# Transposes of q and k for the unit three ahead, issued behind the transposes of x

## The chip, the cores and the metric

The kernel runs on one core of one Trainium2 chip. The core has five engines that run side by side, each through its own queue in order: TensorE (PE in the profile, with PEld for its weight loads), VectorE (DVE), ScalarE (ACT), GpSimd (POOL) and SyncE (SP). DMA transfers are issued by POOL and by SP here and are carried out by 16 DMA engines. The metric is the device time of one execution in microseconds, the median of several runs.

## The reference

Chunked attention on q, k and v of shape (8 batches, 8 heads, 576 positions, 64), with every chunk of 64 positions attending to itself alone, and then a gated feed-forward layer on the 4608 x 512 result:

```
scores = q_c @ k_c.T / sqrt(64)            # per batch, head and chunk: 64 x 64
attn   = softmax(scores)
x      = (attn @ v_c)   -> 4608 x 512      # tokens x (heads * 64)
h      = x @ w_in                          # 512 -> 2048
g      = h * sigmoid(beta * h)
out    = g @ w_out                         # 2048 -> 512, float32
```

## The kernel before

The 4608 tokens are cut into 18 units of 256. Two units make a block of 512, so there are nine blocks, and the loop over `j` from 1 to 8 goes through what is called stage j here. Stage j computes the hidden layer of block j (`emit_m`, 16 column groups, matmuls on L366), the output products of block j - 1 (`emit_prod`, L583; seven products in two halves each instead of eight, with sums of operands formed on VectorE by `emit_sum`, L430), and the attention of later units. In stages 3, 4 and 5 it is the attention of three units each: 8 to 10, 11 to 13, 14 to 16. Unit 17 follows in stage 6.

For each unit u the attention has these steps:

- `load_unit(u)`: POOL issues the loads of q and k of the unit (L104, tiles `qu` and `ku`, four buffers each) and of v (L118, tile `vbig`, a ring of sixteen parts). The loads convert float32 to float16.
- `emit_T(u)`, called T(u) below: for u >= 8, two DMA transposes on SP (L157), `kT<-ku` and then `qT<-qu`; the tiles kT and qT have three buffers each. At its end it calls `loads_to(u + 4)`, so the load of unit u + 4 is put on POOL's queue; that load overwrites the buffers that T(u) reads.
- `emit_sc(u)`, called sc(u): the score matmuls (L217) read qT and kT, then ScalarE takes the exponential (L223).
- `emit_pv(u)`: matmuls with v (L254).
- `emit_norm(u, s)` in two halves: reciprocals and products on VectorE (L286, L288, L276) and two small activations on ScalarE (L287) give x in float16 (`x16`, two buffers).
- `emit_xt_dma(u, s)`, called xt(u) for the two halves: a DMA transpose on SP each (L342, `xt<-x`) into the block's tile `xt`. `emit_m` of block j reads the transposed x of both units 2j and 2j + 1. So the first `emit_m` of stage 4 reads xt(8) and xt(9).

The outputs leave by DMAs on SP as well (L537, `out_dram<-osb`). ScalarE copies a product out of PSUM into one of four `osb` buffers (L600), VectorE adds a second product to it (L603), and `flush_stores` puts the store on SP's queue at the end of the next product. A copy that reuses a buffer waits until the buffer's earlier store has landed.

All of it is issued under a manual schedule: no planner moves anything. Each stage fills a list `items` of (place, priority, step), sorts it by place and then priority, and calls the steps in that order; each engine then works through its own part of the program in this order, and each instruction waits on semaphores for its inputs and for the buffer that it overwrites. The places are fractions of a stage. `ATT` gives for each unit its start a0 and its width w, and `att_items` makes the places of its steps out of them. In stage 3 the three units have a0 = 0.02, 0.35 and 0.68 and w = 0.33:

```
3: ((8, 0.02, 0.33), (9, 0.35, 0.33), (10, 0.68, 0.33)),
```

A step's place orders it among all the steps of its stage; on SP what counts is the order among the transposes and the stores alone. An SP instruction that waits holds up all that is behind it on SP.

Of the kernel before, what the change touches and what calls it, by code (L numbers as in the profile page):

```python
# [15 lines left out]
def kernel(  # L16
# [595 lines left out]
    with tc.manual_schedule():  # L612
# [96 lines left out]
        def att_items(u, a0, w):  # L709
            it = [(a0, 2, ("sc", u)), (a0 + 0.36 * w, 3, ("pv", u)), (a0 + 0.361 * w, 3, ("norm", u, 0)),  # L710
                  (a0 + (0.42 if u >= WV else 0.50) * w, 3, ("norm", u, 1))]
            if u >= WV:
                it.append((a0 + 0.005, 3, ("T", u + 3)))
            return it

        ATT = {2: ((6, 0.36, 0.27), (7, 0.60, 0.27)),
# [12 lines left out]
        for j in range(1, NB):  # L729
# [19 lines left out]
            else:  # L749
# [28 lines left out]
                for i, p in enumerate((1, 2, 6, 5, 7, 3, 4)):  # L778
                    for t in range(2):
                        w = 1.06 if j == NB - 1 else 0.98  # L780
# [15 lines left out]
                for u, a0, w in ATT.get(j, ()):  # L796
                    items += att_items(u, a0, w)
# [86 lines left out]
```

## Time and profile before

| | |
|---|---|
| time, median of 3 runs | 286.99 us (284.39 to 287.27) |
| the profiled execution | 286.72 us, span 284.9 us |
| mean granted TensorE clock | 0.975 |
| PE busy | 269.6 us (95%) |
| VectorE busy | 208.1 us (73%) |
| ScalarE busy | 165.1 us (58%) |
| GpSimd busy | 96.9 us (34%) |
| DMA packets' share, GpSimd's queue / SP's queue | 81.1% / 34.9% |
| PE waiting for `xt<-x` | 3.6 us, once |
| first product of stage 3, 4, 5, 6 on PE | 98.47, 127.40, 162.53, 192.32 us |

The span runs from the first to the last instruction, and the execution's time has 1.8 us around it. Times within the profile are microseconds from the start of the span. In the rows of the forty slices each digit is a share in tenths, for 7.1 us; PEclk is the clock granted to TensorE in tenths of full speed. The queues' shares are of the time of all 16 DMA engines; they can add up to more than 100%, since an engine can have packets of both queues under way. In a list in order of time a line gives the start, the length, the engine, the line of the program, the operation, what it writes and reads, and how many instructions are merged; in brackets the idle time before it and what ended it. A DMA's line on SP or POOL is the time of issuing it; its landing comes later and is given as the time from the start of the issue.

### The profile page before, as it was taken

To read this page: it belongs to the slowest core of one execution; us is meant where nothing else is said; L and a number is where in the kernel's file an instruction comes from. 1 tells how busy PE (TensorE), PEld (TensorE's weight loads), DVE (VectorE), ACT (ScalarE), POOL (GpSimd) and SP (SyncE) were. 2 spreads that over 40 slices of the span, in tenths; PEclk is the share of its full clock that TensorE was granted. 3 is DMA by queue.
4 is the path that set the end of the run, shared out by engine and by line. 5 is a ranking of instruction groups with operands and counts; after the bars stand their busy time and mean duration, and the time that the engine had idled before them with its cause. 6 is when DMAs were issued, how large, how long until landed. Compare 5 with 4: busy or idle time off the path is not lost.

```text
span 284.9 us, 7719 instructions
## 1 busy us (share of the span) xinstructions
PE 269.6 (95%) x3186; PEld 184.6 (65%) x3186; DVE 208.1 (73%) x389; ACT 165.1 (58%) x295; POOL 96.9 (34%) x124
## 2 busy tenths in 40 slices
PE   6589999899999999994999999999999999999995
PEld 2466445656756566662566666666787887788874
DVE  3557666799987587663676687669997989696961
ACT  3358506886555565652456565656657576848721
POOL 8864579489538709432434300000000000000000
PEclk9959999999999999996899999999999999999999
DMA  9999999999999999999999999623412102110223
GB/s 142 174 196 204 181 180 179 241 164 157 141 137 137 173 185 162 153 176 156 192 151 169 157 160 231 132 25 100 66 37 76 37 2 74 39 37 3 74 75 112
DMA packets 145955, 36.95 MB, mean 130 GB/s; under 512 B 130048, under 2 KB 145408, under 8 KB 145920
## 3 DMA queue, kind: packets, MB, share of 16 engines
q0 software_dynamic: 101216, 18.10, 81.1%
q1 hardware_dynamic: 44704, 18.37, 34.9%
q8 instruction: 25, 0.41, 0.6%
q14 instruction: 10, 0.08, 0.1%
HBM read 36.71 MB, written 9.44 MB: 162 GB/s over the span
## 4 chain that ended last, share of the span: by engine, by line
PE 59%; DMA 18%; DVE 10%; POOL 4%; ACT 4%; issue 3%; DVEq 0%; ACTq 0%; POOLq 0%
PE hps L366 22%; PE ya L583 12%; PE yb L583 10%; DMA ku<-in_k_dram 6%; DMA wout<-in_moe_w_out_dram 5%; PE acc L583 5%; PE qx L479 3%; ACT hq L511 3%; DMA win<-in_moe_w_in_dram 3%; PE qz L479 3%; DMA xt<-x 3%; DVE gt L354 2%; DVE gt L525 2%; POOL vbig L118 2%; PE sc L217 1%
## 5 line engine op out<-in xcount | busy, mean ns | idle before, releaser
L366 PE MATMUL hps<-xt,win 128*128 128x512 f16 (+1 forms) x504 | 114.5, 365 | 5.6 <-DMA xt<-x 3.6
L354 DVE SCALAR_TENSOR_TENSOR gt<-sg,hps 128x512 f16<-128x512 f32 (+1 forms) x113 | 69.1, 617 | 44.1 <-ACT sg L378 43.5
L378 ACT ACTIVATE sg<-hps,bt 128x512 f32<-128x512 f32 (+1 forms) x113 | 71.1, 635 | 49.6 <-PE hps L366 48.6
L366 PEld LDWEIGHTS <-win 128*128 128x128 f16 x504 | 49.2, 100 | 40.2 <-DMA xt<-x 3.9
L583 PEld LDWEIGHTS <-sm 128*128 128x128 f16 x512 | 49.3, 98 | 12.3 <-issue 0.3
L583 PEld LDWEIGHTS <-gt 128*128 128x128 f16 x384 | 37.1, 99 | 10.5 <-DVE gt L525 0.6
L118 POOL DMA_DIRECT2D vbig<-in_v_dram x40 | 34.1, 871 | 17.9 <-DMA ku<-in_k_dram 5.3
L104 POOL DMA_DIRECT2D qu<-in_q_dram x22 | 18.7, 861 | 25.9 <-DMA qT<-qu 9.2
L583 PE MATMUL ya<-wt,sm 128*128 128x256 f16 x200 | 26.0, 273 | 0.0
L104 POOL DMA_DIRECT2D ku<-in_k_dram x22 | 18.8, 872 | 11.8 <-DMA ku<-in_k_dram 6.1
L525 DVE TENSOR_SCALAR gt<-hq,rb 128x512 f16<-128x512 f32 x32 | 14.5, 482 | 7.5 <-ACT hq L511 6.5
L430 DVE TENSOR_TENSOR sm<-gt 128x2048 f16<-128x2048 f16 (+1 forms) x17 | 19.7, 1156 | 0.3
L511 ACT ACTIVATE hq<-hq,bs 128x256 f32<-128x256 f32 (+1 forms) x32 | 17.1, 611 | 1.8 <-DVE hq L504 1.8
L600 ACT COPY osb<-ya 128x512 f32<-128x512 f32 x18 | 10.6, 587 | 8.0 <-PE ya L583 7.6
L391 PE MATMUL ops<-wout,gt 128*128 128x512 f16 x64 | 14.5, 379 | 0.0
L583 PE MATMUL ya<-wout,gt 128*128 128x256 f16 x104 | 14.3, 284 | 0.0
L583 PE MATMUL yb<-wout,gt 128*128 128x256 f16 x104 | 13.9, 273 | 0.2
L239 ACT ACTIVATE et<-sc 128x1024 f16<-128x1024 f32 (+1 forms) x9 | 7.3, 833 | 11.4 <-PE sc L230 11.4
L479 PEld LDWEIGHTS <-ws 128*128 128x128 f16 x128 | 12.5, 98 | 2.0 <-issue 0.6
L583 PE MATMUL yb<-wt,sm 128*128 128x256 f16 x104 | 13.5, 273 | 0.1
L583 PE MATMUL yb<-wout,sm 128*128 128x256 f16 x104 | 13.5, 273 | 0.0
L375 ACT ACTIVATE sg<-hps,bs 128x512 f32<-128x512 f32 x13 | 8.8, 687 | 7.2 <-PE hps L366 7.2
(99 smaller groups left out, 344.4 us busy)
## 6 DMA issues: line engine op xcount, KB each, us to landing
out_dram<-osb SPq DMA_DIRECT2D x32, 256.0 KB, 3.0
vbig<-in_v_dram POOLq DMA_DIRECT2D x32, 128.0 KB, 8.0
qu<-in_q_dram POOLq DMA_DIRECT2D x20, 128.0 KB, 5.8
ku<-in_k_dram POOLq DMA_DIRECT2D x20, 128.0 KB, 7.1
win<-in_moe_w_in_dram POOLq DMA_DIRECT2D x8, 256.0 KB, 9.1
wout<-in_moe_w_out_dram POOLq DMA_DIRECT2D x4, 512.0 KB, 12.2
qu<-in_q_dram POOLq DMA_DIRECT2D x4, 256.0 KB, 6.3
ku<-in_k_dram POOLq DMA_DIRECT2D x4, 256.0 KB, 7.2
```

The lines of the kernel that those rows point to most:

```text
L104: nc.gpsimd.dma_start(out=tv[off:off + n, sp], in_=src[b, :, s:s + n, :].rearrange("h p d -> p h d"),)
L118: nc.gpsimd.dma_start(out=vbig[off:off + n, i % NV, :, 0:D], in_=v[b, :, s:s + n, :].rearrange("h p d -> p h d"),)
L354: nc.vector.scalar_tensor_tensor(out=gt_t[j][:, m, c0:c0 + n], in0=sg[:, 0:n], scalar=1.0, in1=hps[:, 0:n], op0=ALU.add, op1=ALU.mult,)
L366: nc.tensor.matmul(out=hps[:, 0:n], lhsT=w_in16[m // 2][:, kk, (m % 2) * 128:(m % 2) * 128 + 128], rhs=xr[:, c0 // CH:(c0 + n) // CH, 2 * ...
L378: nc.scalar.activation(out=sg[:, 0:n], in_=hps[:, 0:n], func=ACTF.Tanh, scale=bt[:, m:m + 1])
L391: nc.tensor.matmul(out=ops, lhsT=gt_t[j][:, kk, t * 128:(t + 1) * 128], rhs=w_out16[kk // 4][:, kk % 4, :], start=(kk == 0), stop=(kk == K ...
L430: nc.vector.tensor_tensor(out=sm[i][:, lo:hi, :], in0=a, in1=b, op=op)
L479: nc.tensor.matmul(out=dst[:, s, :], lhsT=lhsT, rhs=rhs, start=(p in (1, 2, 5) and s == 0 and kk == 0), stop=(s == 1 and kk == 1), skip_gr ...
L511: nc.scalar.activation(out=o, in_=src, func=ACTF.Silu, scale=bs[:, m:m + 1])
L525: nc.vector.tensor_scalar(out=gt_t[j][:, m, :], in0=hq[:, b].rearrange("p c q -> p (c q)"), scalar1=rb[:, m:m + 1], scalar2=None, op0=ALU. ...
L583: nc.tensor.matmul(out=dst, lhsT=lhsT, rhs=rhs, start=(p in (1, 2, 5) and kk == 0 and (t == 0 or last)), stop=(kk == 7 and (t == 1 or last ...
L600: nc.scalar.copy(out=o, in_=acc)
```

## The change

For units from 8 on (`WV` is 8), `att_items` puts T(u + 3) at another place of the list: at a0 + 0.45 w instead of a0 + 0.005. Before, that is just behind sc(u), which is at a0. Now it is behind the second half of the norm, at a0 + 0.42 w, and so behind the two xt(u), which are issued along with the halves of the norm.

```
             it = [(a0, 2, ("sc", u)), (a0 + 0.36 * w, 3, ("pv", u)), (a0 + 0.361 * w, 3, ("norm", u, 0)),
                   (a0 + (0.42 if u >= WV else 0.50) * w, 3, ("norm", u, 1))]
             if u >= WV:
-                it.append((a0 + 0.005, 3, ("T", u + 3)))
+                it.append((a0 + 0.45 * w, 3, ("T", u + 3)))
             return it
```

It concerns T(11) to T(17), which are issued by units 8 to 14; T(8), T(9) and T(10) are issued in stage 2, at places of their own. The order of the instructions on TensorE and on GpSimd is the same as before, and so is that on VectorE and ScalarE. On SP the order from T(10) on, with "st" for a store, is:

```
before: T10 T11 st xt8 st T12 xt9 T13 st xt10 st T14 st xt11 st T15 xt12 T16 st xt13 st T17 st xt14 st xt15 ...
after:  T10 st xt8 T11 st xt9 T12 st xt10 T13 st st xt11 T14 st xt12 T15 st xt13 T16 st st xt14 T17 st xt15 ...
```

More of the change, by code (lines that the diff above doesn't have):

```diff
@@ L712, in att_items @@
             if u >= WV:
-                it.append((a0 + 0.005, 3, ("T", u + 3)))
+                it.append((a0 + 0.45 * w, 3, ("T", u + 3)))
             return it
```

## The prediction

> **What bounds the kernel now.** I read the page first: its busy line and its forty slices, then the costliest groups, then the waits, then single stretches.
>
> ```profile
> PE 269.6 (95%) x3186; PEld 184.6 (65%) x3186; DVE 208.1 (73%) x389; ACT 165.1 (58%) x295; POOL 96.9 (34%) x124
> ...
> PEclk9959999999999999996899999999999999999999
> DMA  9999999999999999999999999623412102110223
> ...
> L366 PE MATMUL hps<-xt,win 128*128 128x512 f16 (+1 forms) x504 | 114.5, 365 | 5.6 <-DMA xt<-x 3.6
> ```
>
> PE is busy for 95% of the span, so only its gaps and its clock can be won. After the start the clock row dips once, in slices 19 and 20, and the group that reads x transposed (L366) has one long wait, 3.6 us for the transpose `xt<-x`. The DMA row is full until slice 25. The instructions in order of time on PE (start, length, line, operation, count, [idle before]) place the wait:
>
> ```profile
> 126.53 1.03 PE L366 MATMUL hps<-xt,win 128*128 128x512 f16 x4
> 127.40 1.04 PE L583 MATMUL ya<-wout,gt 128*128 128x256 f16 x8
> 132.01 1.89 PE L366 MATMUL hps<-xt,win 128*128 128x512 f16 x4 [3.58 <-DMA xt<-x]
> ```
>
> 127.40 is the first product of stage 4; the next matmul is the stage's first `emit_m`, which needs x of units 8 and 9, and it takes 1.89 us where its like takes 1.03. Busy time by stretches gives the clock:
>
> ```profile
> core 0: us, PE busy (x) PEld busy (x) DVE busy (x) ACT busy (x) POOL busy (x), PEclk, DMA share, GB/s
> ...
> 128.00:133.00 5.00, 1.42 (x7) 0.57 (x6) 1.92 (x2) 0.34 (x1) 1.59 (x3) 0.75 1.74 155
> 133.00:138.00 5.00, 5.00 (x79) 2.49 (x76) 1.82 (x2) 2.43 (x4) 1.57 (x2) 0.57 1.73 172
> ```
>
> A clock of 0.5 from 130.5 to 137.3 makes these means (2.5 of 5 us, then 4.3 of 5). The same view in order of time on SP shows why xt was late:
>
> ```profile
> 100.67 2.38 SPq L157 DMA_TRANSPOSE kT<-ku  x1
> 103.15 3.53 SPq L157 DMA_TRANSPOSE qT<-qu  x1
> 106.86 2.29 SPq L157 DMA_TRANSPOSE kT<-ku  x1
> 109.31 1.56 SPq L157 DMA_TRANSPOSE qT<-qu  x1
> 110.97 0.54 SPq L537 DMA_DIRECT2D out_dram<-osb  x1
> 111.61 3.57 SPq L342 DMA_TRANSPOSE xt<-x  x2
> 115.27 0.54 SPq L537 DMA_DIRECT2D out_dram<-osb  x1
> 115.97 3.96 SPq L157 DMA_TRANSPOSE kT<-ku  x1
> 120.03 3.26 SPq L157 DMA_TRANSPOSE qT<-qu  x1
> 123.38 2.67 SPq L342 DMA_TRANSPOSE xt<-x  x2
> ```
>
> These are T(10), T(11), a store, xt(8), a store, T(12), xt(9), where T(u) is kT and qT of unit u. SP runs back to back. VectorE finished x of unit 9 at 116.0 (its L276 pair: 114.86 + 1.15), yet xt(9) was issued at 123.4, behind T(12); its second half, issued at 124.8, landed 7.2 us later, at 132.0.
>
> **The price of that stall.** From first product to first product, stage 3 takes 127.40 - 98.47 = 28.93 us and stage 4 162.53 - 127.40 = 35.13. Stage 5 takes 29.79, of which 0.86 is the next stage's first `emit_m`, which comes ahead of the product there: 28.93 again. So stage 4 loses 6.20 us. That is 3.58 of idle PE, and 137.3 - 132.0 = 5.3 us at half clock, which loses 2.65: together 6.23.
>
> **The change, part by part.** No instruction is added or removed, and PE and POOL keep their order. On SP the seven pairs T(11) to T(17) go from just behind sc(u) to just behind the two xt of unit u.
>
> *xt(9), the gain.* After T(10) (end 106.7) come the store, ready long before, and xt(8), whose x was ready at 105.0 and 107.9: 107.4 to 111.0. T(11) follows, 4.0 us as now, then a store of 0.54: 115.6. x(9) is ready at 116.0, so xt(9) goes at 116.1, its second half at 117.5, and at 7.2 us it lands at 124.7. It is wanted at 128.27, behind the first product. Were T(11) as slow as T(12) now (7.3 us) and the landing that of xt(8) (9.1), it would be 129.4, 1.1 us late. So the idle and, with it, the half clock go: -6.2 us.
>
> *The T pairs, now later.* SP does the same work, so I start each where it started before, plus what now goes ahead of it: T(11) 106.86 + xt(8) 3.57 + store 0.54 = 111.0; T(12) + xt(9) 2.67 and 0.2 of waiting = 118.9; T(13) + xt(10) and a store = 130.0; T(14) + xt(11) and a store of 1.1 = 141.6; T(15) + xt(12) = 150.9; T(16) + xt(13) and a store = 163.7; T(17) + xt(14) and a store = 173.6. With each pair's own lead of kT (1.4 to 4.1 us) and its qT's time from issue to landing in the rows of that tile (7.7, 9.6, 8.4, 9.5, 9.5, 10.0, 4.6 us), they land at 121.2, 132.6, 141.7, 153.8, 163.7, 175.1 and 180.5. The score matmuls (L217) that read them stand now at 133.83, 144.2, 153.9, 164.4, 173.1, 182.8 and 193.3; the first comes at 129.2 without the stall, the others 6.2 earlier: 138.0, 147.7, 158.2, 166.9, 176.6, 187.1. Slack is 8.0, 5.4, 6.0, 4.4, 3.2, 1.5 and 6.6 us, so I take no cost. What hides them is PE's own work between T's issue and sc; where that fails, PE waits at sc. The worst landing of the trace, 10.0 us, is already in unit 16's sum; SP slower by 1 us per unit would make unit 16, five units on, 5 - 1.5 = 3.5 us late, my upper end. There is no gain below nothing, since PE waits for no qT from unit 8 on.
>
> *The loads behind them.* POOL's load of unit 15 overwrites what T(11) reads: it waited until 120.12 for an earlier load, and qT(11) now lands at 121.2, 1.1 us later. Load 14 is in flight until 131.7 (its last ku issued at 113.9, 17.8 us to landing), so the queue doesn't run dry: 0, or at most 1.1 us at ku(15), which lands at 147.1 and has 3.8 us before T(15) at 150.9. The last ku of unit 16 lands at 160.3, ahead of T(16) in the new order too; the later loads have their T landed well before POOL reaches them.
>
> *Stores behind the T.* Store of the third product's sum in stage 3 goes behind T(13), at 136.0, lands 6.8 later at 142.8; ScalarE reuses the buffer at 150.2 - 6.2 = 144.0. The one of stage 4 goes behind T(16), 169.7 as now, lands at 175.7 and is wanted at 179.1 - 6.2 = 172.9: ScalarE's copy stands 2.8 us. Behind it stand tanh activations; `emit_m` has four PSUM buffers 1.74 us apart and needs one about 2.7 us, so 4.2 us of cover. I take 0; uncovered it costs up to 2.8.
>
> *Sum.* The profiled execution took 286.72 us (span 284.9 and 1.8 around it), 0.1% under the median of 286.99. 286.72 - 6.2 = 280.5.
>
> **A rule that speaks against it.** T(12) held SP for 7.3 us (115.97 to 123.29). The Trainium skill (DMA: Bandwidth & Descriptors, Latency and other measured facts) gives a DMA transpose 261 GB/s. For the 2 x 262 KB of one pair that is an estimate of 2.0 us; moving it would then bring xt(9) forward by 2.0 only, leave 1.6 us of idle and, if the clock stays up, give 286.72 - 2.0 - 2.65 = 282.1. With the loads running the trace has the longer time, and the trace decides. On the clock, the trace shows half rate from 2.1 us into a gap of 3.58. The Trainium skill (TensorE: Matmul & The Clock Gate, Why this matters for your kernels) asks for no PE gaps over about 3 us; by it a rest of 1 us of the gap would cost 1 us and no clock.
>
> **Rivals.**
> 1. *Partly given back*, 281.5 to 284.5: xt(9) 1.1 late, or qT(15) and qT(16) late by 1 to 3 us, or ScalarE's 2.8 us coming through. For it: slack of 1.5 at unit 16 and SP without idle. Against it: SP stood 2.4 us at 158 for ku(16), which the new order fills with xt(13).
> 2. *Nothing measurable*, 284.5 to 288: xt(9) arrives at 124 to 128, but the 6.2 us are lost again before 187, since DMA and not PE sets the pace from 106 to 172. Or the executions before vary with the clock alone: 287.0 - 2.65 = 284.4, the lowest of the three, would be the same stall at full clock.
> 3. *Slower*, about 291: SP's pace per unit grows because T, later, competes with the loads. From T(12) to T(15) it is now 32.19 / 3 = 10.7 us, PE's is 28.93 / 3 = 9.64. At 12.5 T(16) would start at 111.0 + 5 x 12.5 = 173.5, land at 184.9, 8.3 us after sc(16) wants it, and with one half clock of 2.65 the sum is 280.5 + 11 = 291.5. At P us per unit the lateness is 111.0 + 5 P + 11.4 - 176.6, and with the half clock it decides from P = 12.2 on (6.8 + 2.65 = 9.45, so 290). Against it: SP's work is the same, and the last load, issued at 160.9, lands 11.2 later, at 172.
> That the change does nothing is excluded: SP's order differs at T(11).
>
> **Numbers.** Forecast 0.63 (279.4 to 281.5), rival 1 0.20, rival 2 0.08, rival 3 0.09. About 1% is what a measurement of this kernel can tell from no change, so faster is 0.83, same 0.08, slower 0.09. The range takes in rival 1: 279.3 to 284.5.
>
> **What would show it.** In the new profile: no `xt<-x` wait on PE, no second clock dip, stage 4 at 28.9 to 29.5 us, xt(9) issued near 116, T(11) near 111. Wrong, if L217 waits for qT at units 14 to 16, or if the load of unit 15 starts after 125.

## The result, and the profile after

The changed kernel takes 282.11 us (median of 15 runs, 279.38 to 284.43) against 286.25 us for the kernel before (15 runs beside them, 282.36 to 287.45). The ratio is 0.9898, with a 95% interval of 0.9856 to 0.9939: 1.0% faster, by 0.6 to 1.4%. (Ratios here leave out executions more than 1.5% above the fastest of their kernel, medians do not, so the two can differ a little.) The profiled execution took 282.26 us, with a span of 280.5. That is 4.46 us less than the profiled execution of before, while the ratio stands for 2.9 us of 286.25: the two profiles lie further apart than the runs do on the whole.

First the page, in the lines that answer to those of before: busy time, the slices of clock and DMA, and the hidden matmuls' group with its idle time in front.

```profile
PE 268.1 (96%) x3186; PEld 184.4 (66%) x3186; DVE 207.6 (74%) x389; ACT 164.4 (59%) x295; POOL 96.9 (35%) x124
...
PEclk9979999999999999999999999999999999999999
DMA  9999999999999999999999999964212102110223
...
L366 PE MATMUL hps<-xt,win 128*128 128x512 f16 (+1 forms) x504 | 111.7, 358 | 1.1 <-DVE gt L354 0.5
```

The second dip of the clock is gone, and so is the wait of L366 for `xt<-x`: 1.1 us of idle time are left of 5.6. The matmuls of L366 take 111.7 us instead of 114.5; none in stage 4 runs at half clock any more, and the dip at the start of the span is shorter as well (slice 3 reads 7 instead of 5). Where PE stands now is seen in its instructions in order of time, at the start of stage 4 and some 10 us into stage 5:

```profile
126.49 1.04 PE L583 MATMUL ya<-wout,gt 128*128 128x256 f16 x8
127.36 1.03 PE L366 MATMUL hps<-xt,win 128*128 128x512 f16 x4
...
155.42 1.04 PE L583 MATMUL ya<-wout,gt 128*128 128x256 f16 x8
...
165.07 1.03 PE L366 MATMUL hps<-xt,win 128*128 128x512 f16 x4
168.46 0.45 PE L217 MATMUL sc<-qT,kT 64*64 64x64 f16 x32 [2.37 <-DVE gt L354]
...
187.86 1.04 PE L583 MATMUL ya<-wout,gt 128*128 128x256 f16 x8
```

The first hidden matmul of stage 4 follows its product without a gap. Stage 4 takes 155.42 - 126.49 = 28.93 us, 6.20 less than before. But the scores of unit 15 stand for 2.37 us, and stage 5 takes 32.44 instead of 29.79. With the two stages' changes, -6.20 and +2.65, go -0.91 up to the first product of stage 3 (97.56 against 98.47) and +0.06 behind 187.86: -4.40, which is the difference of the spans. The -0.91 is no effect of the change: the first transpose that moved is T(11), in stage 3, and the 0.91 us are there by 52 us already (the same matmuls, L323, begin at 51.31 and at 52.22). What the change did in this pair of executions is -6.20 + 2.65 = -3.55 us.

The view names VectorE as what ended that gap. SP's instructions in order of time, and the landing of the one qT in question, say otherwise (SP's list is shown in two stretches):

```profile
106.98 3.48 SPq L342 DMA_TRANSPOSE xt<-x  x2
110.63 2.40 SPq L157 DMA_TRANSPOSE kT<-ku  x1
113.20 3.14 SPq L157 DMA_TRANSPOSE qT<-qu  x1
116.44 0.53 SPq L537 DMA_DIRECT2D out_dram<-osb  x1
117.07 3.81 SPq L342 DMA_TRANSPOSE xt<-x  x2
121.04 3.18 SPq L157 DMA_TRANSPOSE kT<-ku  x1
...
150.76 3.70 SPq L342 DMA_TRANSPOSE xt<-x  x2
154.64 3.86 SPq L157 DMA_TRANSPOSE kT<-ku  x1
158.66 2.55 SPq L157 DMA_TRANSPOSE qT<-qu  x1
```

```profile
L157 SPq DMA_TRANSPOSE qT<-qu x1: 2547/2547/2547, 158.7 to 158.7; - x1
...
DMA to landing us min/median/max: 9.7/9.7/9.7
```

xt(9) goes at 117.07, ahead of T(12). Further down the queue T(15) is behind xt(12): its qT is issued at 158.66 and lands 9.7 us later, at 168.4, and the scores start at 168.46. The experiment with T(15) put back tests this reading.

### The profile page after: what moved, and what is told of

It is laid out like the page before. It is cut to its first block, busy times and chain, and to the rows that moved or that the text cites. A ratio compares the mean times of both kernels' runs of the same rounds, so it can differ in the third digit from the quotient of the medians.

```text
span 280.5 us, 7720 instructions
## 1 busy us (share of the span) xinstructions
PE 268.1 (96%) x3186; PEld 184.4 (66%) x3186; DVE 207.6 (74%) x389; ACT 164.4 (59%) x295; POOL 96.9 (35%) x124
## 4 chain that ended last, share of the span: by engine, by line
PE 66%; DVE 14%; ACT 8%; DMA 6%; issue 4%; POOL 2%; ACTq 0%; DVEq 0%; POOLq 0%
PE hps L366 24%; PE ya L583 12%; PE yb L583 9%; PE acc L583 5%; PE ops L391 5%; DVE gt L354 4%; PE qx L479 3%; DMA xt<-x 3%; ACT hq L511 3%; PE qz L479 3%; DMA ku<-in_k_dram 2%; DVE sm L430 2%; ACT sg L378 2%; DVE gt L525 2%; PE sc L230 1%
## 5 line engine op out<-in xcount | busy, mean ns | idle before, releaser
L366 PE MATMUL hps<-xt,win 128*128 128x512 f16 (+1 forms) x504 | 111.7, 358 | 1.1 <-DVE gt L354 0.5
L366 PEld LDWEIGHTS <-win 128*128 128x128 f16 x504 | 48.4, 98 | 34.2 <-issue 1.8
L583 PEld LDWEIGHTS <-gt 128*128 128x128 f16 x384 | 36.7, 98 | 10.2 <-DVE gt L525 0.6
L583 PE MATMUL ya<-wout,gt 128*128 128x256 f16 x104 | 13.5, 273 | 0.0
## 6 DMA issues: line engine op xcount, KB each, us to landing
wout<-in_moe_w_out_dram POOLq DMA_DIRECT2D x4, 512.0 KB, 12.2
```

Source lines behind the costliest of these rows:

```text
L366: nc.tensor.matmul(out=hps[:, 0:n], lhsT=w_in16[m // 2][:, kk, (m % 2) * 128:(m % 2) * 128 + 128], rhs=xr[:, c0 // CH:(c0 + n) // CH, 2 * ...
L583: nc.tensor.matmul(out=dst, lhsT=lhsT, rhs=rhs, start=(p in (1, 2, 5) and kk == 0 and (t == 0 or last)), stop=(kk == 7 and (t == 1 or last ...
```

## The experiments

Eleven more runs were made, one of them of the changed kernel again. They were made in three sets, each beside the kernel before, so runs of different sets are compared by their ratios. The theory at the start: the gain is xt(9) getting ahead of T(12), and the 2.4 us are the price of the later T. The first four take this apart.

### Only T(12) moved

```
-                it.append((a0 + 0.45 * w, 3, ("T", u + 3)))
+                it.append((a0 + (0.45 * w if u == 9 else 0.005), 3, ("T", u + 3)))
```

> The changed kernel with one T alone moved: T(12) is issued behind xt(9), all other T stand where they stood before. Theory (the gain is xt(9) getting ahead of T(12); the 2.4 us wait of the scores of unit 15 in the changed kernel is the price of moving the later T): xt(9) issued near 116, no wait for xt on PE at 128, stage 4 at 28.9 us, qT(15) lands near 161, so no wait of the scores of unit 15; about 2.4 us faster than the changed kernel, 279.5 to 281, with a store then landing up to 4 us after ScalarE wants its buffer. Rival (all T must be late to free SP for the xt): xt(9) later than 118 and part of the stall at 128 is back, 283 to 286.

285.25 us against 285.69, ratio 0.9944 (0.9901 to 0.9986). The start was as expected: xt(9) was issued at 115.22, PE had no gap at 128 and no score matmul waited as long as half a microsecond.

```profile
115.22 4.58 SPq L342 DMA_TRANSPOSE xt<-x  x2
119.97 2.77 SPq L157 DMA_TRANSPOSE kT<-ku  x1
```

The time was not. ScalarE's instructions in order of time show four long waits for DMAs in stages 4 and 5:

```profile
141.49 0.59 ACT L600 COPY osb<-ya 128x512 f32<-128x512 f32 x1 [3.27 <-DMA out_dram<-osb]
...
155.82 0.52 ACT L287 ACTIVATE x<-xe,rx 128x64 f16<-128x64 f32 x2 [4.08 <-DMA xt<-x]
...
166.44 0.52 ACT L287 ACTIVATE x<-xe,rx 128x64 f16<-128x64 f32 x2 [3.57 <-DMA xt<-x]
...
175.51 0.59 ACT L600 COPY osb<-ya 128x512 f32<-128x512 f32 x1 [4.02 <-DMA out_dram<-osb]
```

They are waits for buffers. A copy into `osb` waits until the store that reads the buffer has landed, and the norm of unit u until xt(u - 2) has read its `x16`. PE's gaps in the two stages are 1.61, 0.34, 0.81, 0.70, 0.40 and 2.11 us, 5.97 in all: nearly all that the start of stage 4 had brought. So the loss is elsewhere now: with T early it is the stores and the xt that are late. A new question came up, whether the buffers or the DMAs themselves are the limit.

### All but T(12) moved

```
-                it.append((a0 + 0.45 * w, 3, ("T", u + 3)))
+                it.append((a0 + (0.005 if u == 9 else 0.45 * w), 3, ("T", u + 3)))
```

> The changed kernel with T(12) put back in front of xt(9), all other T late as in the change. Theory: xt(9) is issued behind T(12) near 122 and lands near 131, PE waits about 3 us at the start of stage 4 with a dip of the clock or without, and since PE is that much later the scores of unit 15 wait less: 284 to 287, no faster than the kernel before by over 1%. Rival (the gain comes from the later T, through DMA contention, and not from xt(9)): stays within 0.5% of the changed kernel, 281 to 283.5.

287.85 us against 285.69, ratio 1.0084 (1.0043 to 1.0125): slower than before, and 0.85 us above the expected range. xt(9) goes at 122.53, behind T(12), and PE's list has the old gap, longer than before. SP and PE:

```profile
122.53 2.58 SPq L342 DMA_TRANSPOSE xt<-x  x2
```

```profile
132.20 1.89 PE L366 MATMUL hps<-xt,win 128*128 128x512 f16 x4 [5.30 <-DMA xt<-x]
```

It is followed by a dip of the clock, and there is no other gap in stages 4 and 5. So the place of this one T against xt(9) makes or undoes the gain; moving the other six without it gains nothing.

### T(15) back in front of xt(12)

```
-                it.append((a0 + 0.45 * w, 3, ("T", u + 3)))
+                it.append((a0 + (0.005 if u == 12 else 0.45 * w), 3, ("T", u + 3)))
```

> The changed kernel with T(15) alone put back to its earlier place, in front of xt(12). Theory (PE stands 2.4 us at the scores of unit 15 because qT(15) lands at 168.4): T(15) is issued about 3.7 us sooner, near 151, qT(15) lands near 164, the wait is gone: 2 to 2.4 us faster than the changed kernel, near 280. Rival (the wait is for VectorE, as the view of waits names it, or SP falls behind all the same): a wait of 1.5 us or more remains at the scores of unit 15 or moves to unit 16, time within 0.3% of the changed kernel.

287.03 us against 285.69, ratio 1.0035 (0.9996 to 1.0074): no faster than before, and worse than the changed kernel. The first half came as expected: T(15) at 150.21, and no wait at the scores of unit 15. But xt(12) now went at 157.95, and the norm of unit 14 waits for it. ScalarE and then PE, in order of time:

```profile
167.97 0.52 ACT L287 ACTIVATE x<-xe,rx 128x64 f16<-128x64 f32 x2 [8.38 <-DMA xt<-x]
```

```profile
168.33 1.86 PE L366 MATMUL hps<-xt,win 128*128 128x512 f16 x4 [5.51 <-ACT x L287]
```

PE stands 5.51 us, and its next matmuls run at half clock. Both the theory and the rival put the loss in the wrong place. That qT(15) makes the changed kernel's wait is confirmed by its vanishing; that the wait could be had back by swapping two entries was wrong.

### The gap filled with matmuls, in the kernel before

```
+            if j == 4:
+                items.append((0.01, 0, ("idle", 15)))
             items.sort(key=lambda it: it[:2])
...
+                elif it[0] == "idle":
+                    emit_idle(it[1], 512)
```

> The kernel before with 15 matmuls of 512 columns on a constant tile put at the start of stage 4, behind the first product and in front of the first hidden matmul, 15 x 0.216 = 3.2 us; the output does not depend on them. Theory (of the 6.2 us that stage 4 loses, 3.6 are idle PE and 2.6 the half clock that follows): PE stays at full clock through 128 to 138, the first hidden matmul still starts at about 132, stage 4 takes 32.5 to 33 us instead of 35.1, and the time falls by 2 to 2.6 us, to about 284. Rival (the dip of the clock is no consequence of the gap, or does not cost anything): the clock dips all the same, stage 4 at 35 us and the time unchanged.

283.04 us against 285.69, ratio 0.9928 (0.9885 to 0.997). PE's list at the start of stage 4, and the busy time by stretches, whose last three columns are clock, DMA share and GB/s:

```profile
127.99 1.04 PE L583 MATMUL ya<-wout,gt 128*128 128x256 f16 x8
128.87 3.40 PE L610 MATMUL warm<-idle 128*128 128x512 f16 x15
132.40 1.04 PE L366 MATMUL hps<-xt,win 128*128 128x512 f16 x4
```

```profile
128.00:133.00 5.00, 4.86 (x27) 2.45 (x26) 1.91 (x2) 0.69 (x1) 1.82 (x3) 1.00 1.72 132
133.00:138.00 5.00, 5.00 (x93) 3.11 (x91) 3.37 (x7) 3.31 (x7) 1.56 (x2) 1.00 1.75 164
```

xt(9) is as late as ever, the work starts at 132.4, but at full clock. Stage 4 takes 160.47 - 127.99 = 32.48 us, 2.65 less than the 35.13 of before. This is the price of the half clock, measured by itself; the other 3.6 us of the 6.2 are idle time. Over all runs the difference is 2.65 us by the medians and 2.1 us by the ratio.

### Less for the DMA engines to do

The changed kernel without ten of the v loads: the products of units 13 to 17 use v of eight units before, so the output of these units is another one. Nothing else changes.

```
         load_qk(u)
+        if u >= 13:
+            return
         load_v(2 * u)
```

> The changed kernel without the v loads of units 13 to 17: their output products use the v that lies in the ring from eight units before, so those units of the output are not the reference's; all instructions on TensorE, VectorE, ScalarE and SP stay. Theory (from 106 to 172 the 16 DMA engines set the pace of SP's transposes, 11 us per unit, and qT of unit 15 is late for that): the T and xt are issued and land faster, T(12) to T(16) follow each other by less than 10.3 us, the scores of unit 15 wait 0 to 0.5 us and the time falls 2 to 2.5 us below the changed kernel's, to about 279.5 to 280.5. Rival (SP's own cost of issuing a transpose is the pace): still 10.8 to 11 us per unit, the 2.4 us wait stays, 282.

280.07 us against 286.19, ratio 0.9804 (0.974 to 0.9868). These are four executions, from 279.26 to 283.28, and the interval touches that of the changed kernel; the profile decides. SP issues T(12) and T(15) here (the line numbers are two higher in this kernel):

```profile
120.36 3.08 SPq L159 DMA_TRANSPOSE kT<-ku  x1
...
150.97 2.70 SPq L159 DMA_TRANSPOSE kT<-ku  x1
```

From T(12) to T(15) that is 10.2 us per unit, where the changed kernel has (154.64 - 121.04) / 3 = 11.2; up to T(16) it is 9.8 against 11.1. PE has no gap in stages 4 and 5, and they take 28.93 and 29.79 us. The transposes are the same instructions in the same order; with less load traffic they are issued and land sooner. So SP's pace goes with the load traffic and is not a fixed cost of issuing. The rows of T(16) have it plainly; the last load, issued at 144.8, landed at most 9.6 us later:

```profile
159.56 1.23 SPq L159 DMA_TRANSPOSE kT<-ku  x1
160.90 1.27 SPq L159 DMA_TRANSPOSE qT<-qu  x1
```

1.23 and 1.27 us, where the changed kernel's T(16) took 3.58 and 2.90.

### T(12) alone, with more buffers

```
-    osb_p = ctx.enter_context(tc.tile_pool(name="osb", bufs=4))
+    osb_p = ctx.enter_context(tc.tile_pool(name="osb", bufs=5))
...
-                (("vb", 1), ("qk", 4), ("qt", 3), ("et", 3), ("rd", 2), ("x16", 4))]
+                (("vb", 1), ("qk", 4), ("qt", 3), ("et", 2), ("rd", 2), ("x16", 4))]
...
-            x16 = x_p.tile([128, 2, 2, 4, D], FP16, tag="x32", name="x16", bufs=2)
+            x16 = x_p.tile([128, 2, 2, 4, D], FP16, tag="x32", name="x16", bufs=3)
...
-                it.append((a0 + 0.45 * w, 3, ("T", u + 3)))
+                it.append((a0 + (0.45 * w if u == 9 else 0.005), 3, ("T", u + 3)))
```

The constant tile for the matmuls at the start goes from 512 to 448 columns, to make room.

> Only T(12) moved, behind xt(9), and more buffers: three instead of two for x16 of units from 8 on, five instead of four for the stores' osb; paid for by two instead of three buffers for the exponentials and a narrower constant tile for the matmuls at the start. Theory (with only T(12) moved the losses in stages 4 and 5 are waits for the two x16 buffers, 4.1 and 3.6 us on ScalarE, and for the osb buffers, 3.3 and 4.0 us; T itself is early enough): these waits vanish, stages 4 and 5 take 29 to 30 us each, time 279.5 to 281.5, 2% under the kernel before. Rival (DMA pace: the late xt and stores just become late for somebody else, the hidden matmuls or the scores): 283 to 286, with waits of PE for xt or qT in stages 4 and 5.

279.34 us (278.49 to 280.23) against 286.19, ratio 0.9755 (0.9713 to 0.9798): the fastest of all, 2.4% under the kernel before, and about 1.4% under the changed one by the two ratios. The first products of stages 4, 5 and 6 on PE:

```profile
126.23 1.04 PE L583 MATMUL ya<-wout,gt 128*128 128x256 f16 x8
...
155.16 1.04 PE L583 MATMUL ya<-wout,gt 128*128 128x256 f16 x8
...
184.96 1.04 PE L583 MATMUL ya<-wout,gt 128*128 128x256 f16 x8
```

28.93 and 29.80 us: no gap is left in either stage. ScalarE waits once, 1.42 us for a store, at no cost. SP is not faster here: from T(12) at 117.24 to T(15) at 149.31 it takes 10.7 us per unit, as in the kernel before. The transfers are late for nobody, because the buffers let the norm and the copies go on.

### The third x16 buffer with T(15) put back

The order of the kernel with T(15) back, with three x16 buffers and two for the exponentials.

> The kernel with T(15) put back in front of xt(12), and three x16 buffers instead of two (two instead of three for the exponentials). Theory (there x16 of unit 14 waits for xt(12), 8.4 us on ScalarE, and PE stands 5.5 us for it with a dip of the clock; the scores of unit 15 don't wait any more): with the third buffer that wait vanishes, PE has no gap over 1 us in stages 4 and 5, time 279.5 to 281. Rival (DMA pace): the gap moves to the scores of unit 15 or 16 or to the osb copies and 2 us or more remain: 282 to 284.

281.62 us against 286.19, ratio 0.9845 (0.9802 to 0.9887). The 8.4 us wait of the norm is gone, and the ratio falls from 1.0035 to 0.9845: in that order it was the buffer. One gap of PE over 1 us is left, against the expectation: 1.99 us up to 128.65, in front of stage 4's first hidden matmul. The view names VectorE for it. But xt(9) was issued at 118.15 in this execution, its second half at 119.50, and that landed 9.0 us later, at 128.5: this is what came too late. The clock did not dip. ScalarE's 3.98 us for a store, until 177.39, are followed by a gap of 0.38 on PE.

### The buffers with the order of the change

> The changed kernel with the three x16 and five osb buffers (and two for the exponentials). Theory (in the changed kernel the waits of ScalarE for a store, 2.8 and 3.5 us, and for x16, 1.2 us, cost PE nothing; what costs is the 2.4 us of qT(15)): ScalarE's waits vanish, the wait at the scores of unit 15 stays at 2 to 3 us, time within 0.3% of the changed kernel. Rival (the ScalarE waits cost as well, or delay xt(12) and so T(15)): the wait at unit 15 shrinks below 1.5 us, 280 to 281.

281.38 us against 286.19, ratio 0.9838 (0.979 to 0.9885), 0.6% under the changed kernel's ratio, with intervals that overlap. ScalarE has no wait left for a store or for xt. PE waits for qT twice:

```profile
158.15 0.44 PE L217 MATMUL sc<-qT,kT 64*64 64x64 f16 x32 [1.47 <-DMA qT<-qu]
...
167.64 0.45 PE L217 MATMUL sc<-qT,kT 64*64 64x64 f16 x32 [0.65 <-DMA qT<-qu]
```

2.12 us in all, at units 14 and 15, where the changed kernel had 2.37 at unit 15. The expected 2 to 3 us at unit 15 did not come: 0.65 us there is less than the rival's 1.5, but the 1.47 us at unit 14 are new. So these buffers don't remove the wait in this order: it is qT that is late, and here the view names it. Whether they save the 0.6% can't be told.

### The changed kernel once more

> The changed kernel once more, unchanged, to stand on one chip beside the two that follow. Theory (the gap at the start of stage 4 is gone, and what the DMA pace takes back in stage 5 differs from execution to execution): 281 to 283, no wait for xt at 128, one or two waits of 1 to 3 us in all in stages 4 and 5. Rival (the 2.4 us at the scores of unit 15 are fixed by the order on SP): the same wait of 2.2 to 2.6 us at the same place.

283.41 us against 285.73, ratio 0.9886 (0.9843 to 0.993), the same as the first time within the intervals, and 0.4 us above the expected range. The profile fell on its longest execution, 285.5 us. It has one gap, and after it the clock dips:

```profile
168.93 0.64 PE L217 MATMUL sc<-qT,kT 64*64 64x64 f16 x32 [2.96 <-DMA qT<-qu]
```

```profile
165.00:170.00 5.00, 2.04 (x41) 1.15 (x39) 3.27 (x5) 1.09 (x3) 0.00 (x0) 0.82 1.55 159
170.00:175.00 5.00, 5.00 (x20) 2.80 (x19) 0.69 (x1) 1.92 (x3) 0.00 (x0) 0.50 1.52 186
```

The same place, as the rival said, but with 2.96 instead of 2.37 us: 0.6 us more of idle time, and the half clock on top. Of the 3.24 us between the two profiled executions stage 5 has 191.00 - 155.30 - 32.44 = 3.26. So how much is lost at unit 15 varies, and whether the clock follows varies with it.

### The buffers without the reordering

> The kernel before with the three x16 and five osb buffers (and two for the exponentials), order unchanged. Theory (before, the only loss is xt(9) behind T(12); the buffers matter only once that is gone): xt(9) issued near 123, PE waits 3 to 4 us at the start of stage 4, time within 0.7% of the kernel before. Rival (the buffers alone make the 279.3 of the kernel with T(12) moved): 280 to 283.

285.87 us against 285.73, ratio 0.9988 (0.9948 to 1.0028): nothing. xt(9) goes at 121.75, behind T(12), and PE stands 4.36 us for it at the start of stage 4:

```profile
131.47 1.08 PE L366 MATMUL hps<-xt,win 128*128 128x512 f16 x4 [4.36 <-DMA xt<-x]
```

The buffers are worth something only once that gap is gone.

### T(12) alone, with the third x16 buffer only

> Only T(12) moved, three x16 buffers, but four osb buffers as before. Theory (of the 6 us that the kernel with T(12) alone moved lost in stages 4 and 5, x16 and osb each have a part): ScalarE waits for stores by 3 to 4 us as it did there, PE stands 1 to 3 us in all behind them; 280.5 to 283, between 285.3 and 279.3. Rival (x16 alone was the cause): 279 to 280.2, no gap of PE over 0.5 us in stages 4 and 5.

286.31 us against 285.73 by the medians, ratio 0.9949 (0.9888 to 1.0011): no difference that can be told; the executions go from 281.69 to 288.0. In the profiled one, 285.99 us, the waits for x16 are gone, but the four `osb` buffers hold ScalarE longer than foreseen, and PE behind it:

```profile
173.16 0.58 ACT L600 COPY osb<-ya 128x512 f32<-128x512 f32 x1 [5.77 <-DMA out_dram<-osb]
```

```profile
175.10 1.86 PE L366 MATMUL hps<-xt,win 128*128 128x512 f16 x4 [4.11 <-DVE gt L354]
```

4.11 us of idle time and a dip of the clock. So the third x16 buffer alone does not make the 279.3, and the fifth `osb` buffer is needed. Whether that one alone would do isn't shown: no run has five `osb` and two x16 buffers.

## Why the prediction was right or wrong

**The sign and the range held; the forecast itself did not come, the first rival did.** The forecast was 280.5 at a chance of 0.63; 282.1 lies in the rival "partly given back", 281.5 to 284.5, which had 0.20. The range held because it was drawn to take in this rival. One of the prediction's own signs of being wrong came too: L217 waits for qT at unit 15.

**The stall and its price** were right to the hundredth in the profiled executions. Stage 4 takes 28.93 us, as the neighbours' 28.93 said. Its two parts were measured apart: filling the gap saves 2.65 us of stage 4, the rest is idle time. That T(12) is the one that matters was argued from SP's list; moving it alone removes the gap, putting it back alone restores it. But the executions of the kernel before are not all like the profiled one, as the prediction's second rival suspected. Of the 35 executions beside the first four experiments, the 15 up to 284.6 us have a mean granted clock of 0.986 to 1.000, and 15 of the 20 longer ones have 0.982 or less; two dips of 6.8 us, as in the profile, make 0.975, and two executions at 1.000 had none. Against executions without that dip the gain can't be 6.2 us at the start of stage 4, which may be part of why the ratio shows less than the profiled pair. Which executions dip in stage 4, the runs' mean clocks don't show.

**xt(9)** was to go at 116.1 and land at 124.7. It went at 117.07, because T(11) took 5.7 us of SP and not the 4.0 of before. Its second half, issued at 119.17, landed 7.6 us later, at 126.8, and was in time for 127.36. The margin was 0.6 us, not the 3.6 foreseen (124.7 against 128.27): with xt(9) issued at 118.15, in the order with T(15) back and three x16 buffers, PE stood 1.99 us.

**The step that failed is the start of the T pairs: "SP does the same work, so I start each where it started before, plus what now goes ahead of it."** That took a transpose's time on SP as a property of the transpose. The starts were foreseen and measured as follows:

| | T(11) | T(12) | T(13) | T(14) | T(15) | T(16) | T(17) |
|---|---|---|---|---|---|---|---|
| foreseen, us | 111.0 | 118.9 | 130.0 | 141.6 | 150.9 | 163.7 | 173.6 |
| measured, us | 110.63 | 121.04 | 132.07 | 143.55 | 154.64 | 165.36 | 176.28 |

By T(15) SP is 3.7 us behind the estimate. Ahead of it, the five xt from 8 to 12 take 17.8 us to issue where they took 15.3 before, and the pairs T(11) to T(14) 24.4 instead of 22.9 (from the start of kT to the end of qT). All seven xt from 8 to 14 take 24.0 instead of 20.5, and 25.1 in the second profile of the changed kernel. So qT(15) lands at 168.4, not 163.7, and the slack of 3.2 us becomes a wait of 2.4. The kernel without ten v loads shows what sets the pace: with less load traffic the same list runs at 10.2 instead of 11.2 us per unit, and the wait is gone. The length of an issue on SP went with what else the DMA engines had to carry. The second rival named the mechanism, "DMA and not PE sets the pace from 106 to 172", at a chance of 0.08, and the third a growing pace of SP; it belonged in the forecast's own sum. Why the same transposes take longer in the new order than in the old isn't shown: the bytes are the same.

The thinnest slack was put at unit 16 (1.5 us), and the wait came at unit 15. With that delay on PE, qT(16), landed at 177.1, was in time for its scores at 178.1.

**Stores behind the T.** In stage 5 the copy was to stand 2.8 us, hidden by four PSUM buffers. It stood 3.51 us, and PE behind it 0.16: hidden, as costed. In stage 4 no wait was foreseen, since the store was to land at 142.8 and the buffer to be wanted at 144.0; the copy stood 2.80 us there, until 146.00, and with five `osb` buffers it does not. It cost PE nothing. The cover was smaller than the 4.2 us worked out, though. This copy, out of yb, covers 3.4 to 3.6 us (3.51 - 0.16, and 3.98 - 0.38 with T(15) back and three x16 buffers). The one out of ya covers 1.7 to 1.9 (3.27 - 1.61, 4.02 - 2.11 and 5.77 - 4.11 in the orders with T(12) alone). These are differences of a wait and the gap that follows it, not costs measured by themselves.

**Loads.** Load 15 was to start 1.1 us later, 121.2. It started at 123.23, since qT(11) was issued at 113.20 and took 9.5 us; nothing came of it that the trace shows.

**The third rival** (291, from 12.2 us per unit on) stayed away: the pace grew from 10.7 to 11.2, not to 12.2. But a late transfer on SP reaches further than I put it. With T(15) back, SP's order costs 5.5 us of idle time through x16, a path that the prediction did not list at all.

**The rule on the transposes' rate** (Trainium skill, DMA: Bandwidth & Descriptors, Latency and other measured facts) gives the pair an estimate of 2.0 us; the page's figure is for a middle dimension that is not contiguous. Beside the loads a pair, T(11) to T(16), took 5.5 to 6.5 us of SP in the changed kernel (its two rows added), so the rule fails at this place. Without loads it held SP for 2.5 us (1.23 + 1.27), near the estimate; but the second of these transposes landed 4.2 us after its issue, so at what rate the data moved no run here shows. **The rule on gaps** (Trainium skill, TensorE: Matmul & The Clock Gate, Why this matters for your kernels), to stay under about 3 us, agrees with these profiles: gaps of 1.99, 2.11 and 2.37 us left the clock up, 2.96, 3.58, 4.11, 4.36, 5.30 and 5.51 us brought it down.

## What to carry to other kernels

Put the transfer that somebody waits for soonest ahead on its queue, and when a stall is taken away, ask at once which buffers are freed by DMAs: here two pools with one buffer too few turned a 6 us gain into anything from nothing to all of it, by the order chosen. While the DMA engines are full, don't carry over the time that a transfer took on its queue from one order to another; bound it with the slowest row of its kind. A short gap of TensorE can cost nearly double through the clock (3.58 us of idle time and 2.65 behind it), so filling it with matmuls on a constant tile was worth 2.65 us without a change in what was late.

## What the runs showed of the hardware that was not expected

- The time that SP needs to issue one 128x1024 DMA transpose is not its own: 1.23 us when no loads run (T(16) without ten v loads), 2.2 to 4.2 us while they do (T(11) to T(16) of the changed kernel), in the same order of instructions. Single issues of 1.3 to 1.6 us occur beside loads too, as at 160.48 and 109.31 in the kernel before.
- Less for one DMA queue sped up the other. Without ten v loads SP's pace from T(12) to T(16) went from 11.1 to 9.8 us per unit.
- A dip has no fixed length. Taken as a clock of 0.5, it lasts 6.8 us in the kernel before (clock 0.75 and 0.57 over 128 to 133 and 133 to 138), and 3.4 us in the same order with more buffers, after a longer gap of 4.36 us (0.93 and 0.73 over the same stretches).
- Two executions of the same kernel with gaps of 2.37 and 2.96 us at the same instruction differ by 3.3 us in the stage, with the clock at 1.00 after the first and 0.50 after the second (170 to 175).
